# Weight sums rounded one piece later, and both plain products first in the first Strassen branch

## The chip, the cores and the metric

The kernel runs on one core of a Trainium2 chip, as one program. Its time is the device time in microseconds. The times of the kernel before are 688.67, 688.81 and 691.49 us, median 688.81; about half a per cent is what a measurement of it can tell from no change. Engines are called as in the profile: PE (matmul), DVE (VectorE), ACT (ScalarE), POOL (GpSimd) and SP, which issues the loads. Each works through its own queue in order, and semaphores tie them together.

## The reference

Three layers, one after the other, on 1152 tokens of 512 features:

```
q_pool = mean of pairs of q rows;  attn = softmax(q_pool k^T / 8) v      2 x 8 heads, 1152 x 64
h = x @ w_in;  g = elu(h);  x = g @ w_out                                512 -> 2048 -> 512
xn = x / rms(x) * rms_g                                                  last layer from here
out = (silu(xn @ w_gate) * (xn @ w_val)) @ w_out                         512 -> 1536 -> 512
```

The weights come as float64 and nearly float32 accuracy is kept.

## The kernel before, in words

Every float32 operand is split into a high part (rounded to the format that PE reads) and a low part (the rest), and a product is three matmuls: high by high, high by low, low by high (`product`, `group`). Activations lie transposed, features on the partitions, in three chunks `c` of 384 tokens; a PSUM bank holds 128 features of one chunk. Seven banks are used in turn.

**Weight pieces.** All weight matrices are read as one stream of pieces of 128 x 512 numbers (`Stream`). One piece goes through SP (load `wr`, two buffers), ACT (`we`, `wm`: two passes over the words of the float64), DVE (three passes that clamp, shift and join them into `wt`; L123, L125, L128), ACT again (high part `wh`, L176) and POOL (low part `wl`, L64). `Stream.work` is a generator; each `ws.step(i, k)` in the main program issues up to k more of these instructions between the matmuls, and so sets their place in each engine's queue. `wm` has a single PSUM bank, so ACT's next `wm` waits for DVE's `wt`.

**Gate and value products.** The last layer's first two products are made of 24 pieces, numbered 32 + 2n and 33 + 2n for n from 0 to 11; even n are gate, odd n value. n = 0 and 1 are multiplied plainly (`unit`). From n = 2 each pair of pieces is one `Branch`: chunks 0 and 1 together go through a Strassen-Winograd scheme with seven products m1 to m7 of half the depth (6 matmuls each, `group`, L707), and chunk 2 plainly, as m8 and m9 (12 matmuls each, `product`, L209 to L211). That is 66 matmuls. m3, m5, m6 and m7 read sums and differences of the four quarters of the pair: `combine` makes them on POOL (four adds into `sf`), `round` gives their high part on ACT (`sh` or `tsh`, L163) and their low part on POOL (`sl` or `tsl`, L64). In the trace `tsh` and `tsl` are a shared tile; they hold sums of pairs 3, 4, 6, 7 and so on beside differences of the activations.

DVE makes `u2` = m6 + m1 (L754) and `u3` = that + m7, still on the bank (L759); m7 is accumulated on m6's bank and so has to wait for `u2`, and m4 on m7's and has to wait for `u3`. The results go through silu on ACT (gate) or a multiplication on DVE (value, L717).

**Order.** `run` gives the order of the products by a list, with 3 steps of the stream behind each m1 to m7 and 6 behind m8 and m9. The first branch runs m1, m8, m6, then m5, m9, m7, m2; later ones are interleaved with what is left of the branch before. Ahead of the branches stand the norm of chunk 2 (`norms[2]`: `spread` transposes a reciprocal on PE, L633; `scale` on DVE, L639, with the parts `xh` on ACT and `xl` on POOL and DVE) and the four plain units.

The names in the rows: `b` is a bank, `u` a result or an add's output, `m` the copy of m1, `sf` a sum, `ts` and `s` its parts, `x` the activations.

Of the kernel before, what the change touches and what calls it, by code (L numbers as in the profile page):

```python
# [39 lines left out]
def tile_kernel(ctx: ExitStack, tc: tile.TileContext, qd, kd, vd, w1d, w2d, wgd, wvd, wod, rgd, outd):  # L40
# [33 lines left out]
    class Stream:  # L74


        def __init__(self, srcs):
            self.srcs = srcs
            self.loaded = self.done = self.at = 0
            self.alloc = False  # L80
            self.bank = self.late = None
            self.pairs_from, self.pairs, self.limit, self.pair = len(srcs), 0, 0, None
            self.raw, self.parts, self.sums = {}, {}, {}
            self.pools = [(wp, NE)]
            self.ops = self.work()
# [14 lines left out]
        def work(self):  # L100
            tail = None
            for i in range(len(self.srcs)):
                if tail and not wide:
                    yield from tail
                self.load(i + 2)
                w = self.raw.pop(i)
                if wide:

                    lo, hi = w[:, :, 0], w[:, :, 1]
                    e = wp.tile([128, 512], U32, tag="we", name="we", bufs=2)
                    w = wp.tile([128, 512], U32, tag="wt", name="wt", bufs=3)
                    t = self.bank.tile([128, 512], U32, tag="wm", name="wm", bufs=1) if self.bank else w
                    T.activation(out=e, in_=lo, func=AF.Copy, scale=0.93625 * 2.0 ** -29)
                    yield
                    T.activation(out=f(t), in_=f(hi), func=AF.Abs, scale=2.0 ** 16)  # L119
                    yield  # L120
                    if tail:
                        yield from tail
                    V.tensor_scalar(out=f(t), in0=f(t), scalar1=LEAST64, scalar2=MOST64, op0=ALU.max, op1=ALU.min)  # L123
                    yield
                    V.scalar_tensor_tensor(out=t, in0=t, scalar=3, in1=e,  # L125
                                           op0=ALU.logical_shift_left, op1=ALU.bitwise_or)
                    yield
                    V.scalar_tensor_tensor(out=w, in0=hi, scalar=0x80000000, in1=t,  # L128
                                           op0=ALU.bitwise_and, op1=ALU.bitwise_xor)
                    self.load(i + 3)  # L130
                    yield
                    w = f(w)
                if self.late:
                    yield from self.late
                    self.late = None
                tail = self.split(i, w)
                n, odd = divmod(i - self.pairs_from, 2)
                if 2 <= n < self.pairs:
                    tail = chain(tail, self.combine(n, even, w)) if odd else tail
                    even = w  # L140
                yield
            yield from tail

        def combine(self, n, a, b):

            sf = mp.tile([128, 4, 256], F32, tag="sf", name="sf", bufs=1)
            s1, s2, s3, s4 = (sf[:, k] for k in range(4))
            a11, a12, a21, a22 = a[:, 0:256], a[:, 256:512], b[:, 0:256], b[:, 256:512]
            G.tensor_tensor(out=s1, in0=a21, in1=a22, op=ALU.add)
            yield  # L150
            G.tensor_tensor(out=s2, in0=s1, in1=a11, op=ALU.subtract)
            yield
            G.tensor_tensor(out=s3, in0=a11, in1=a21, op=ALU.subtract)
            yield
            G.tensor_tensor(out=s4, in0=a12, in1=s2, op=ALU.subtract)
            self.late = self.round(n, sf.rearrange("p s (k c) -> p (s k) c", k=2))

        def round(self, n, sf):
            self.pair = n
# [53 lines left out]
    def xchunk(c):  # L213
        return lambda k: (xh[:, k, cs(c)], xl[:, k, cs(c)])
# [3 lines left out]
    def flush():  # L218
        while pending:
            pending.pop(0)()  # L220
# [230 lines left out]
    for n in range(ns):  # L451
        p, k = n // NPT, n % NPT
# [71 lines left out]
    for step in range(ns):  # L524
# [20 lines left out]
        for u in jobs.get(step, []):  # L545
            do_prep(u, (ACT[0], lo_pool) if step < 4 and u[0] != "q" else POOL)
            n = order.index(u)
# [40 lines left out]
    def bank():  # L588

        nonlocal nbank  # L590
        n, nbank = nbank % 7, nbank + 1
        if n == 5 and len(psb) == 1:
            with tc.using_default_side("right"):
                psb.append(ctx.enter_context(tc.tile_pool(name="psC", bufs=2, space=PSUM)))
                ws.bank = ctx.enter_context(tc.tile_pool(name="psW", bufs=1, space=PSUM))
        return psb[n >= 5].tile([128, 512], F32, tag="b", name="b", bufs=2 if n >= 5 else 5)[:, 0:CH]
# [47 lines left out]
    norms = [Norm(c) for c in range(3)]  # L644
# [3 lines left out]
    for hf in range(2):  # L648
# [30 lines left out]
        if hf:  # L679
            T.activation(out=dummy, in_=eps, func=AF.Sqrt)  # L680
            for c in range(3):
                for n in range(4):
                    m, q = 2 + n // 2, n % 2
                    if q == 0:
                        b = bank()
# [10 lines left out]
    class Branch:  # L696


        def __init__(self, n):
            self.n, self.val = n, n % 2  # L700
            self.i = 2 * (n // 2)
            self.w = [ws.get(wi + 2 * n + k) for k in range(2)]

# [6 lines left out]
        def out(self, k, c, p, add=None, into=None):  # L710
# [7 lines left out]
            else:  # L718
                pending.append(lambda: T.activation(out=d, in_=p, func=AF.Silu))

        def m(self, n):
            w = self.w
            a11, a12, a22 = ([t[:, 2 * j:2 * j + 2] for t in w[i]] for i, j in ((0, 0), (0, 1), (1, 1)))
            b11, b21, b22 = ([t[:, 2 * j:2 * j + 2, cs(l)] for t in (xh, xl)] for j, l in ((0, 0), (1, 0), (1, 1)))
            s = lambda k: [t[:, 2 * k - 2:2 * k] for t in ws.get_sums(self.n)]
            if n == 1:
                self.a = bank()
                self.group(self.a, a11, b11, True, False)
                self.m1 = hp.tile([128, CH], F32, tag="e", name="m1", bufs=4)
                T.copy(self.m1, self.a)  # L730
                flush()
            elif n == 2:
                self.group(self.a, a12, b21, False, True)
                flush()
                self.out(0, 0, self.a)
                self.out(1, 1, self.e, self.u3, self.a)
            elif n == 3:
                self.group(self.e, s(4), b22, False, True)
                flush()
                self.out(0, 1, self.e, self.u2)  # L740
            elif n == 4:
                self.group(self.b, a22, ts[3], False, True)
                flush()
                self.out(1, 0, self.b, self.m1)
            elif n == 5:
                self.e = bank()
                self.group(self.e, s(1), ts[0], True, False)
                flush()
            elif n == 6:
                self.b = bank()  # L750
                self.group(self.b, s(2), ts[1], True, False)
                flush()
                self.u2 = hp.tile([128, CH], F32, tag="e", name="u2", bufs=4)
                V.tensor_tensor(out=self.u2, in0=self.b, in1=self.m1, op=ALU.add)  # L754
            elif n == 7:
                self.group(self.b, s(3), ts[2], False, False)
                flush()
                self.u3 = up.tile([128, CH], F32, tag="u3", name="u3", bufs=2)
                V.tensor_tensor(out=self.u3, in0=self.b, in1=self.m1, op=ALU.add)  # L759
            else:  # L760
                b = bank()
                product(b, w[n - 8], xchunk(2), True, True)
                flush()
                self.out(n - 8, 2, b)

    def unit(i, c, between=None):
        b = bank(), bank()
        for n in range(2):
            product(b[n], ws.get(2 * n + i + wi), xchunk(c), True, True)
            if between and n == 0:  # L770
                between()
        return i, c, *b

    def swiglu(i, c, pg, pv, k=4):
        s = u[c][:, i]
        T.activation(out=s, in_=pg, func=AF.Silu)
        ws.step(wi, k)
        V.tensor_tensor(out=s, in0=pv, in1=s, op=ALU.mult)
# [21 lines left out]
    swiglu(*first[0], 0)  # L800
    lo_pool(ts[1][1], t2, ts[1][0])
    swiglu(*first[1], 2)
    units = [unit(1, 0, norms[2].spread)]
    norms[2].scale()
    lo_pool(ts[3][1], t4, ts[3][0])
    ws.step(wi, 7)
# [17 lines left out]
    def run(order, i, limit, k=3):  # L824
        ws.limit = limit
        for br, m in order:
            br.m(m)
            ws.step(wi + 2 * i, 2 * k if m > 7 else k)
# [15 lines left out]
    old = None  # L844
    for n in range(2, 11):
        b = Branch(n)
        if old:
            run([(b, 1), (old, 4), (b, 6), (old, 3)], n - 1, n + 2)
        else:
            run([(b, 1), (b, 8), (b, 6)], n, n + 2)  # L850
        if n == 10:
            split_u(0, 0, 3)
        run([(b, k) for k in ((5, 8, 7, 2, 9) if old else (5, 9, 7, 2))], n, n + 3)
        old = b
    b = Branch(11)
    run([(b, 1), (old, 4), (b, 6), (old, 3)], 10, 12, 1)
# [86 lines left out]
```

## Time and profile before

| | us |
|---|---|
| median of three runs | 688.81 |
| the profiled execution | 690.5 |
| its span | 688.6 |
| PE busy | 670.8 |
| DVE / ACT / POOL busy | 469.7 / 461.5 / 406.8 |

The span is the time between the first and last instruction that the profile sees; 1.9 us lie around it. Mean granted clock of PE over the span is 0.995 of full speed. In a timeline, the brackets at the end of a row give the idle time ahead of the instruction and what ended it. Matmuls are pipelined: each shows about 0.34 us, but the next starts half that later.

### The profile page before, as it was taken

What the parts mean: (1) busy time and instruction counts of PE and PEld (TensorE: products, weight loads), DVE (VectorE), ACT (ScalarE), POOL (GpSimd) and SP (SyncE); (2) the same over time, 40 slices, a digit from 0 to 9 for tenths busy, and PEclk for the clock granted to TensorE, in tenths of its full rate; (3) what the DMA queues carried; (4) which work ended last, traced back from release to release, by engine and by line L of the source; (5) the groups of instructions that cost most, each with busy time, mean ns of one, the idle gap of its engine ahead of it and who ended that gap; (6) DMA issues with size and microseconds to landing.
All of it is one profiled execution on the core that took longest, in us unless ns stands there. A gap on an engine that the chain in (4) does not pass through costs nothing.

```text
span 688.6 us, 11381 instructions
## 1 busy us (share of the span) xinstructions
PE 670.8 (97%) x4183; PEld 660.3 (96%) x4183; DVE 469.7 (68%) x803; ACT 461.5 (67%) x921; POOL 406.8 (59%) x366
## 2 busy tenths in 40 slices
PE   7999999999999999999999999999798999999997
PEld 6999999999999999999999999999698999999997
DVE  5989989998998966663445665397566866776300
ACT  5978889898988958984558875345655555644300
POOL 5798888888988406772224554376777676323200
PEclk9999999999999999999999999999999999999999
DMA  5522343223242001233222122101333222304200
GB/s 190 192 93 87 123 139 105 96 88 118 88 137 83 1 3 61 93 122 123 93 92 90 64 93 92 62 30 62 105 110 123 89 96 83 102 1 133 89 35 35
DMA packets 21608, 62.34 MB, mean 91 GB/s; under 512 B 2736, under 2 KB 4784, under 8 KB 21552
## 3 DMA queue, kind: packets, MB, share of 16 engines
q1 hardware_dynamic: 21552, 61.62, 27.1%
q8 instruction: 33, 0.54, 0.3%
q14 instruction: 23, 0.19, 0.1%
HBM read 59.25 MB, written 2.36 MB: 89 GB/s over the span
## 4 chain that ended last, share of the span: by engine, by line
PE 85%; POOL 4%; DVE 4%; ACT 3%; issue 2%; DMA 1%; SPq 0%; DVEq 0%; POOLq 0%; ACTq 0%
PE b L209 15%; PE b L211 15%; PE b L210 15%; PE s L321 10%; PE o L365 10%; PE b L707 10%; PE t L339 9%; DMA rawk<-in_k_dram 1%; DVE x L791 1%; POOL kd L64 1%; POOL vd L64 1%; DVE wm L125 1%; ACT xh L640 1%; DVE wm L123 1%; DVE wt L128 1%
## 5 line engine op out<-in xcount | busy, mean ns | idle before, releaser
L64 POOL TENSOR_TENSOR wl<-wt,wh 128x512 fp32r<-128x512 f32 x68 | 91.3, 1342 | 94.2 <-ACT wh L176 94.0
L209 PE MATMUL b<-xh,wh 128*128 128x384 f32 x356 | 120.5, 338 | 3.1 <-DVE u L717 3.1
L211 PE MATMUL b<-xh,wl 128*128 128x384 f32 x356 | 120.3, 338 | 0.0
L210 PE MATMUL b<-xl,wh 128*128 128x384 f32 x356 | 120.2, 338 | 0.0
L70 DVE TENSOR_TENSOR ptl<-t,pth 128x384 fp32r<-128x384 f32 x216 | 106.6, 548 | 4.4 <-ACT pth L347 3.5
L325 DVE TENSOR_SCALAR_CACHE_REDUCE p<-s 128x1152 f32<-128x1152 f32 x72 | 97.3, 1353 | 17.9 <-PE s L321 17.4
L347 ACT CAST pth<-t 128x384 fp32r<-128x384 f32 x216 | 89.2, 487 | 24.2 <-PE t L339 23.4
L321 PE MATMUL s<-kd,qt 128*128 128x384 f32 x480 | 97.9, 341 | 2.7 <-DVE p L325 1.6
L330 ACT ACTIVATE p<-p,st 128x1152 f32<-128x1152 f32 x72 | 91.5, 1271 | 0.5 <-DVE p L325 0.2
L339 PE MATMUL t<-ident,p 128*128 128x128 f32 x648 | 85.4, 275 | 1.4 <-ACT p L330 0.9
L321 PEld LDWEIGHTS s<-kd,qt 128*128 128x128 f32 x480 | 81.7, 188 | 4.5 <-POOL kd L64 2.0
L365 PE MATMUL o<-pth,vd 128*128 128x256 f32 (+1 forms) x288 | 84.4, 315 | 0.0
L339 PEld LDWEIGHTS t<-ident,p 128*128 128x128 f32 x648 | 73.9, 141 | 7.8 <-DVE ptl L70 4.7
L123 DVE TENSOR_SCALAR wm<-wm 128x512 f32<-128x512 f32 x62 | 43.1, 695 | 52.1 <-ACT wm L119 52.1
L365 PE MATMUL o<-ptl,vd 128*128 128x256 f32 (+1 forms) x288 | 78.4, 294 | 0.0
L209 PEld LDWEIGHTS b<-xh,wh 128*128 128x128 f32 x356 | 67.2, 189 | 3.4 <-DVE u L717 3.4
L210 PEld LDWEIGHTS b<-xl,wh 128*128 128x128 f32 x356 | 67.3, 189 | 0.0
L211 PEld LDWEIGHTS b<-xh,wl 128*128 128x128 f32 x356 | 67.3, 189 | 0.0
L64 POOL TENSOR_TENSOR gl<-e,gh 128x384 fp32r<-128x384 f32 x37 | 38.8, 1053 | 41.1 <-ACT gh L230 39.6
L209 PE MATMUL b<-gh,wh 128*128 128x384 f32 x180 | 60.9, 338 | 0.0
L211 PE MATMUL b<-gh,wl 128*128 128x384 f32 x180 | 60.5, 336 | 0.0
L210 PE MATMUL b<-gl,wh 128*128 128x384 f32 x180 | 60.5, 336 | 0.0
(183 smaller groups left out, 1510.7 us busy)
## 6 DMA issues: line engine op xcount, KB each, us to landing
wr<-in_w_dram SPq DMA_DIRECT2D x32, 512.0 KB, 3.3
rawk<-in_k_dram SPq DMA_DIRECT2D x32, 288.0 KB, 3.0
rawq<-in_q_dram SPq DMA_DIRECT2D x15, 576.0 KB, 4.1
wr<-in_wg_dram SPq DMA_DIRECT2D x12, 512.0 KB, 3.2
wr<-in_wv_dram SPq DMA_DIRECT2D x12, 512.0 KB, 3.2
wr<-in_wo_dram SPq DMA_DIRECT2D x12, 512.0 KB, 3.2
rawv<-in_v_dram SPq DMA_DIRECT2D x16, 288.0 KB, 2.8
out_dram<-o SPq DMA_DIRECT2D x12, 192.0 KB, 1.8
```

Of the source, the lines that this page charges most:

```text
L64: G.tensor_tensor(out=o, in0=i, in1=f(h), op=ALU.subtract)
L70: V.tensor_tensor(out=o, in0=i, in1=f(h), op=ALU.subtract)
L209: PE.matmul(out, lhsT=wh[:, k, :], rhs=ah, start=first and k == 0, stop=False)
L210: PE.matmul(out, lhsT=wh[:, k, :], rhs=al, start=False, stop=False)
L211: PE.matmul(out, lhsT=wl[:, k, :], rhs=ah, start=False, stop=last and k == 3)
L321: PE.matmul(s[:, m, 0:384], lhsT=a, rhs=b[:, 384 * m:384 * m + 384], start=n == 0, stop=n == len(parts) - 1)
L325: V.tensor_scalar(out=pt, in0=s[:, :, 0:384], scalar1=-0.0625, scalar2=None, op0=ALU.mult, op1=ALU.min, accum_out=st[p][:, 0, TILES[i][4], :])
L330: T.activation(out=pt, in_=pt, func=AF.Exp, scale=-1.0, bias=st[p][:, 0, TILES[i][4], :], accum_out=st[p][:, 1, TILES[i][4], :])
L339: PE.transpose(ps[:, k, :], src[:, 128 * b:128 * b + 128], ident)
L347: T.copy(oh, re(ps))
L365: PE.matmul(self.o[:, 0:self.N], lhsT=v[:, b, :], rhs=(pth, ptl)[u][:, g["buf"], b, g["c0"]:320], start=self.n == 0, stop=self.n == 17)
L707: PE.matmul(out, lhsT=a[x][:, k, :], rhs=b[y][:, k, :], start=first and (k, x, y) == (0, 0, 0), stop=last and (k, x, y) == (1, 1, 0), skip ...
```

## The change

Three places. In `Stream`, `combine` leaves its rounding in `next` instead of `late`; the cast to the high part is now issued behind the next piece's tail (its `wh`), and the low part behind that piece's passes on DVE, so that it comes after the previous piece's `wl` on POOL and not before it. In the first branch m9 stands behind m8 in front of m6, and the order m5, 9, 7, 2 is now m5, m2, m7; the output that needs both m2 and m7 is issued when the later one is done (`both`); the next branch's m6 comes ahead of the first branch's m4. And the transposes of the last norm stand behind both products of the unit in which they stood in the middle.

```
@@ -78,7 +78,7 @@
             self.srcs = srcs
             self.loaded = self.done = self.at = 0
             self.alloc = False
-            self.bank = self.late = None
+            self.bank = self.late = self.next = None
             self.pairs_from, self.pairs, self.limit, self.pair = len(srcs), 0, 0, None
             self.raw, self.parts, self.sums = {}, {}, {}
             self.pools = [(wp, NE)]
@@ -102,6 +102,9 @@
             for i in range(len(self.srcs)):
                 if tail and not wide:
                     yield from tail
+                    if self.next:
+                        yield from self.next
+                        self.next = None
                 self.load(i + 2)
                 w = self.raw.pop(i)
                 if wide:
@@ -120,6 +123,11 @@
                     yield
                     if tail:
                         yield from tail
+                    if self.late:
+                        yield next(self.late)
+                        yield next(self.late)
+                    self.late, late = self.next, self.late
+                    self.next = None
                     V.tensor_scalar(out=f(t), in0=f(t), scalar1=LEAST64, scalar2=MOST64, op0=ALU.max, op1=ALU.min)
                     yield
                     V.scalar_tensor_tensor(out=t, in0=t, scalar=3, in1=e,
@@ -130,9 +138,8 @@
                     self.load(i + 3)
                     yield
                     w = f(w)
-                if self.late:
-                    yield from self.late
-                    self.late = None
+                    if late:
+                        yield from late
                 tail = self.split(i, w)
                 n, odd = divmod(i - self.pairs_from, 2)
                 if 2 <= n < self.pairs:
@@ -153,7 +160,7 @@
             G.tensor_tensor(out=s3, in0=a11, in1=a21, op=ALU.subtract)
             yield
             G.tensor_tensor(out=s4, in0=a12, in1=s2, op=ALU.subtract)
-            self.late = self.round(n, sf.rearrange("p s (k c) -> p (s k) c", k=2))
+            self.next = self.round(n, sf.rearrange("p s (k c) -> p (s k) c", k=2))
 
         def round(self, n, sf):
             self.pair = n
@@ -697,7 +704,7 @@
 
 
         def __init__(self, n):
-            self.n, self.val = n, n % 2
+            self.n, self.val, self.half = n, n % 2, 0
             self.i = 2 * (n // 2)
             self.w = [ws.get(wi + 2 * n + k) for k in range(2)]
 
@@ -717,6 +724,11 @@
                 V.tensor_tensor(out=d, in0=p, in1=d, op=ALU.mult)
             else:
                 pending.append(lambda: T.activation(out=d, in_=p, func=AF.Silu))
+
+        def both(self):
+            self.half += 1
+            if self.half == 2:
+                self.out(1, 1, self.e, self.u3, self.a)
 
         def m(self, n):
             w = self.w
@@ -733,7 +745,7 @@
                 self.group(self.a, a12, b21, False, True)
                 flush()
                 self.out(0, 0, self.a)
-                self.out(1, 1, self.e, self.u3, self.a)
+                self.both()
             elif n == 3:
                 self.group(self.e, s(4), b22, False, True)
                 flush()
@@ -757,6 +769,7 @@
                 flush()
                 self.u3 = up.tile([128, CH], F32, tag="u3", name="u3", bufs=2)
                 V.tensor_tensor(out=self.u3, in0=self.b, in1=self.m1, op=ALU.add)
+                self.both()
             else:
                 b = bank()
                 product(b, w[n - 8], xchunk(2), True, True)
@@ -800,7 +813,8 @@
     swiglu(*first[0], 0)
     lo_pool(ts[1][1], t2, ts[1][0])
     swiglu(*first[1], 2)
-    units = [unit(1, 0, norms[2].spread)]
+    units = [unit(1, 0)]
+    norms[2].spread()
     norms[2].scale()
     lo_pool(ts[3][1], t4, ts[3][0])
     ws.step(wi, 7)
@@ -845,12 +859,12 @@
     for n in range(2, 11):
         b = Branch(n)
         if old:
-            run([(b, 1), (old, 4), (b, 6), (old, 3)], n - 1, n + 2)
+            run([(b, 1), (old, 4), (b, 6), (old, 3)] if n > 3 else [(b, 1), (b, 6), (old, 4), (old, 3)], n - 1, n + 2)
         else:
-            run([(b, 1), (b, 8), (b, 6)], n, n + 2)
+            run([(b, 1), (b, 8), (b, 9), (b, 6)], n, n + 2)
         if n == 10:
             split_u(0, 0, 3)
-        run([(b, k) for k in ((5, 8, 7, 2, 9) if old else (5, 9, 7, 2))], n, n + 3)
+        run([(b, k) for k in ((5, 8, 7, 2, 9) if old else (5, 2, 7))], n, n + 3)
         old = b
     b = Branch(11)
     run([(b, 1), (old, 4), (b, 6), (old, 3)], 10, 12, 1)
```

ACT in the first branch, before: `tsh` is the high part of the sums of pair 3, the cast that waits for POOL; `m_5849` is the copy of the first branch's m1.

```order
L176 CAST wh<-wt 128x512
L730 COPY m_5849<-b 128x384
L163 CAST tsh<-sf 128x1024
L117 ACTIVATE we<-wr 128x512
L119 ACTIVATE wm<-wr 128x512
L719 ACTIVATE u_5746<-b 128x384
L176 CAST wh<-wt 128x512
```

And now:

```order
L183 CAST wh<-wt 128x512
L742 COPY m_5849<-b 128x384
L120 ACTIVATE we<-wr 128x512
L122 ACTIVATE wm<-wr 128x512
L183 CAST wh<-wt 128x512
L726 ACTIVATE u_5746<-b 128x384
L170 CAST tsh<-sf 128x1024
```

The cast has moved behind the next piece's `we` and `wm` and the `wh` that follows, and an output's silu.

DVE in the same place, before: three rows are one piece; the adds that take `m_5849` are `u2` and then `u3` of the first branch.

```order
L123 TENSOR_SCALAR wm<-wm 128x512
L125 SCALAR_TENSOR_TENSOR wm<-wm,we 128x512
L128 SCALAR_TENSOR_TENSOR wt<-wr,wm 128x512
L754 TENSOR_TENSOR u_5883<-b,m_5849 128x384
L123 TENSOR_SCALAR wm<-wm 128x512
L125 SCALAR_TENSOR_TENSOR wm<-wm,we 128x512
L128 SCALAR_TENSOR_TENSOR wt<-wr,wm 128x512
L759 TENSOR_TENSOR u_5932<-b,m_5849 128x384
```

And now:

```order
L131 TENSOR_SCALAR wm<-wm 128x512
L133 SCALAR_TENSOR_TENSOR wm<-wm,we 128x512
L136 SCALAR_TENSOR_TENSOR wt<-wr,wm 128x512
L131 TENSOR_SCALAR wm<-wm 128x512
L133 SCALAR_TENSOR_TENSOR wm<-wm,we 128x512
L136 SCALAR_TENSOR_TENSOR wt<-wr,wm 128x512
L766 TENSOR_TENSOR u_5906<-b,m_5849 128x384
L131 TENSOR_SCALAR wm<-wm 128x512
L771 TENSOR_TENSOR u_5943<-b,m_5849 128x384
```

`u2` has gone from behind the first of these pieces to behind the second; between `u2` and `u3` stands one row instead of three.

POOL at the first sums, before: four adds, the sums' low part, two pieces' low parts.

```order
L149 TENSOR_TENSOR sf<-wt 128x256
L151 TENSOR_TENSOR sf<-sf,wt 128x256
L153 TENSOR_TENSOR sf<-wt 128x256
L155 TENSOR_TENSOR sf<-wt,sf 128x256
L64 TENSOR_TENSOR sl<-sf,sh 128x1024
L64 TENSOR_TENSOR wl<-wt,wh 128x512 x2
```

And now:

```order
L156 TENSOR_TENSOR sf<-wt 128x256
L158 TENSOR_TENSOR sf<-sf,wt 128x256
L160 TENSOR_TENSOR sf<-wt 128x256
L162 TENSOR_TENSOR sf<-wt,sf 128x256
L64 TENSOR_TENSOR wl<-wt,wh 128x512
L64 TENSOR_TENSOR sl<-sf,sh 128x1024
L64 TENSOR_TENSOR wl<-wt,wh 128x512
```

The sums' low part stands between the two pieces' low parts.

## Rows read from the trace of the kernel before

**Rows 1.** Page: span, busy times, and PE in 40 slices of 17.2 us

```profile
span 688.6 us, 11381 instructions
...
PE 670.8 (97%) x4183; PEld 660.3 (96%) x4183; DVE 469.7 (68%) x803; ACT 461.5 (67%) x921; POOL 406.8 (59%) x366
...
PE   7999999999999999999999999999798999999997
```

**Rows 2.** Windows: length, busy PE, PEld, DVE, ACT, POOL (count), granted clock, DMA, GB/s

```profile
486.50:490.00 3.50, 3.50 (x22) 3.35 (x20) 3.05 (x6) 1.58 (x4) 2.21 (x3) 1.00 0.45 149
497.67:501.70 4.03, 4.03 (x14) 4.03 (x15) 3.25 (x6) 2.25 (x6) 3.18 (x4) 0.60 0.47 146
540.00:560.00 20.00, 20.00 (x116) 20.00 (x115) 14.05 (x25) 10.67 (x19) 14.53 (x14) 1.00 0.26 89
```

**Rows 3.** PE timeline, 466 to 519: start, length, line, tiles, idle before and releaser

```profile
466.33 0.54 PE L633 MATMUL b<-ident,rr 128*128 128x128 f32 x3 [0.60 <-DVE rr L627]
...
473.17 0.34 PE L210 MATMUL b<-xl,wh 128*128 128x384 f32 x1
...
486.08 0.45 PE L707 MATMUL b<-tsh,sl 128*128 128x384 f32 x1 [1.10 <-POOL sl L64]
...
490.72 0.44 PE L707 MATMUL b<-tsh,sh 128*128 128x384 f32 x1 [0.55 <-DVE u L754]
...
497.67 0.45 PE L707 MATMUL b<-tsh,wh 128*128 128x384 f32 x1 [3.51 <-DVE u L759]
...
518.38 0.44 PE L209 MATMUL b<-xh,wh 128*128 128x384 f32 x1 [3.12 <-DVE u L717]
```

**Rows 4.** Waits of all engines: total us, times, longest

```profile
DVE wm L123 <- ACT wm L119: 52.1, 35, 5.4
```

**Rows 5.** ACT timeline, 482 to 513, first two branches

```profile
484.41 0.63 ACT L119 ACTIVATE wm<-wr 128x512 f32<-128x512 f32 x1
...
492.78 1.05 ACT L163 CAST tsh<-sf 128x1024 fp32r<-128x1024 f32 x1 [3.91 <-POOL sf L155]
...
512.88 1.05 ACT L163 CAST sh<-sf 128x1024 fp32r<-128x1024 f32 x1 [4.31 <-POOL sf L155]
```

**Rows 6.** DVE timeline, 470 to 518

```profile
470.26 2.18 DVE L639 SCALAR_TENSOR_TENSOR x<-x,rg,b 128x384 f32<-128x384 f32 x4
...
478.26 1.42 DVE L70 TENSOR_TENSOR xl<-x,xh 128x768 fp32r<-128x768 f32 x1 [1.51 <-ACT xh L810]
...
481.58 0.69 DVE L128 SCALAR_TENSOR_TENSOR wt<-wr,wm 128x512 uint32<-128x512 uint32 x1
...
486.60 0.69 DVE L128 SCALAR_TENSOR_TENSOR wt<-wr,wm 128x512 uint32<-128x512 uint32 x1
...
494.94 0.70 DVE L123 TENSOR_SCALAR wm<-wm 128x512 f32<-128x512 f32 x1 [4.27 <-ACT wm L119]
...
497.07 0.55 DVE L759 TENSOR_TENSOR u<-b,m 128x384 f32<-128x384 f32 x1
...
517.77 0.56 DVE L717 TENSOR_TENSOR u<-b,u 128x384 f32<-128x384 f32 x1
```

**Rows 7.** POOL timeline, 471 to 504

```profile
471.49 2.31 POOL L64 TENSOR_TENSOR xl<-x,xh 128x384 fp32r<-128x384 f32 x2 [4.77 <-ACT xh L640]
...
478.82 1.46 POOL L149 TENSOR_TENSOR sf<-wt 128x256 f32<-128x256 f32 x1
...
481.75 0.74 POOL L155 TENSOR_TENSOR sf<-wt,sf 128x256 f32<-128x256 f32 x1
483.64 2.38 POOL L64 TENSOR_TENSOR sl<-sf,sh 128x1024 fp32r<-128x1024 f32 x1 [1.16 <-ACT sh L163]
...
496.23 1.27 POOL L64 TENSOR_TENSOR wl<-wt,wh 128x512 fp32r<-128x512 f32 x1
...
503.77 2.41 POOL L64 TENSOR_TENSOR tsl<-sf,tsh 128x1024 fp32r<-128x1024 f32 x1 [1.16 <-ACT tsh L163]
```

**Rows 8.** Loads of the weight pieces, tile wr: issue to landing

```profile
DMA to landing us min/median/max: 3.0/3.2/6.1
```

More of the change, by code (lines that the diff above doesn't have):

```diff
@@ L80, in __init__ @@
             self.alloc = False
-            self.bank = self.late = None
+            self.bank = self.late = self.next = None
             self.pairs_from, self.pairs, self.limit, self.pair = len(srcs), 0, 0, None
@@ L104, in work @@
                     yield from tail
+                    if self.next:
+                        yield from self.next
+                        self.next = None
                 self.load(i + 2)
@@ L122, in work @@
                         yield from tail
+                    if self.late:
+                        yield next(self.late)
+                        yield next(self.late)
+                    self.late, late = self.next, self.late
+                    self.next = None
                     V.tensor_scalar(out=f(t), in0=f(t), scalar1=LEAST64, scalar2=MOST64, op0=ALU.max, op1=ALU.min)
@@ L132, in work @@
                     w = f(w)
-                if self.late:
-                    yield from self.late
-                    self.late = None
+                    if late:
+                        yield from late
                 tail = self.split(i, w)
@@ L155, in combine @@
             G.tensor_tensor(out=s4, in0=a12, in1=s2, op=ALU.subtract)
-            self.late = self.round(n, sf.rearrange("p s (k c) -> p (s k) c", k=2))
+            self.next = self.round(n, sf.rearrange("p s (k c) -> p (s k) c", k=2))
         def round(self, n, sf):
@@ L699, in __init__ @@
         def __init__(self, n):
-            self.n, self.val = n, n % 2
+            self.n, self.val, self.half = n, n % 2, 0
             self.i = 2 * (n // 2)
@@ L719, in out, with both @@
                 pending.append(lambda: T.activation(out=d, in_=p, func=AF.Silu))
+        def both(self):
+            self.half += 1
+            if self.half == 2:
+                self.out(1, 1, self.e, self.u3, self.a)
         def m(self, n):
@@ L735, in m @@
                 self.out(0, 0, self.a)
-                self.out(1, 1, self.e, self.u3, self.a)
+                self.both()
             elif n == 3:
@@ L759, in m @@
                 V.tensor_tensor(out=self.u3, in0=self.b, in1=self.m1, op=ALU.add)
+                self.both()
             else:
@@ L802, in tile_kernel @@
     swiglu(*first[1], 2)
-    units = [unit(1, 0, norms[2].spread)]
+    units = [unit(1, 0)]
+    norms[2].spread()
     norms[2].scale()
@@ L847, in tile_kernel @@
         if old:
-            run([(b, 1), (old, 4), (b, 6), (old, 3)], n - 1, n + 2)
+            run([(b, 1), (old, 4), (b, 6), (old, 3)] if n > 3 else [(b, 1), (b, 6), (old, 4), (old, 3)], n - 1, n + 2)
         else:
-            run([(b, 1), (b, 8), (b, 6)], n, n + 2)
+            run([(b, 1), (b, 8), (b, 9), (b, 6)], n, n + 2)
         if n == 10:
             split_u(0, 0, 3)
-        run([(b, k) for k in ((5, 8, 7, 2, 9) if old else (5, 9, 7, 2))], n, n + 3)
+        run([(b, k) for k in ((5, 8, 7, 2, 9) if old else (5, 2, 7))], n, n + 3)
         old = b
```

## The prediction

> **What bounds the kernel now.** I read the engine totals and the PE slices first. PE is busy 670.8 of 688.6 us and the only slices after the start that are not at 9 are 28 and 30, so from 482 to 534 us; everything before and after them is a full PE [rows 1]. Then the windows: in an undisturbed stretch of the branches 116 matmuls go by in 20 us, 0.1724 us each, at a granted clock of 1.00; behind the longest gap 14 matmuls take 4.03 us at 0.60, a mean over a low part at 1.2 GHz and a rest at 2.4 [rows 2]. Then PE's timeline, for every matmul with an idle time in brackets: the five gaps from the last norm on are 0.60, 1.10, 0.55, 3.51 and 3.12 us, in sum 8.88 [rows 3]. What a low clock adds: 14 matmuls should take 2.41 us, so 1.62 us are lost behind the 3.51 gap; behind the 3.12 gap the trace repeats that (14 matmuls in 4.02 us), 1.61. Together 12.1 us are lost in the stretch that the change touches. There is nothing else on PE to win: a faster side engine is worth only what it takes from these 12.1 us.
>
> Why PE waits there is read one engine back. DVE's wait on `wm` for ACT is a large group, 52.1 us in 35 waits [rows 4]. In ACT's timeline roundings of weight sums wait in turn for POOL's last add; the two that matter have 3.91 and 4.31 us of idle time ahead of them [rows 5]. ACT is strictly in order, so the next piece's `we` and `wm` stand behind the blocked cast; DVE's clamp waits 4.27 us for `wm`, and behind the clamp and its two partners stands the add `u3`, which PE's next group needs: it starts at 497.07 and PE at 497.67 [rows 3, 6]. The 3.12 gap is the same chain: cast 512.88, `u` at 517.77, PE at 518.38 [rows 3, 5, 6]. POOL itself is not full: lower parts of sums two pairs apart start at 483.64 and 503.77, 10.07 us for a pair [rows 7], of which work is four adds at 0.74, one lower part of a sum at 2.4 and two of pieces at 1.27, 7.9 us; the rest is waiting for ACT's rounding. A branch on PE is 66 matmuls, 11.4 us.
>
> **The change, step by step.** No instruction is added or removed; only the order moves, on PE, ACT, DVE and POOL, and SP's loads follow as buffers come free.
>
> *Rounding behind the next piece.* The cast of a sum now comes after the next piece's `we`, `wm` and the current `wh`, so POOL has long finished when ACT reaches it. ACT no longer stands still ahead of it, DVE gets its clamp, and the two long gaps go: 3.51 + 3.12, and with them the low clock, 1.62 + 1.61; 9.86 us in sum. POOL has `wl` to do while ACT rounds, so its 1.16 us wait [rows 7] falls away too, and its pair comes near to 7.9 us.
>
> *Price at the first sum.* The first pair has no lead. `wt` of piece 38 ends at 482.27 [rows 6]; then `wm` of 39 (0.6), `wh` of 38 (0.6), the cast (1.05) [rows 5], while POOL does `wl` of 38; the lower part starts about 484.9 and ends near 487.3, where it ended at 486.02 before [rows 7]. PE asked for it at 484.98 (486.08 less 1.10) and now, with the other plain product of 12 matmuls in front, 2.07 us later, and 0.2 us earlier for the norm: at about 486.85. The gap of 1.10 becomes 0.5; with a wake-up on either engine between I take 0.7, between 0.5 and 0.9. The product in front needs only piece 37 and the next of seven banks in turn, both long free, so it costs nothing itself.
>
> *What is late next: `u2` of the first branch.* This add held PE for 0.55 us before [rows 3]. It now stands on DVE behind piece 41's three instructions too. Chain: `wm` of 39 starts at 482.33, as soon as `wt` of 38 is done; from `wm` to the end of `wt` the rows give 2.88 us (484.41 to 487.29) [rows 5, 6], so `wt` of 39 ends at 485.2. That frees the load buffer for piece 41, which lands 3.2 us later (3.0 to 6.1) [rows 8], 488.5. Then `we` (0.6), `wm` to `wt` (2.88) and the add (0.55): 492.5. PE comes to that group 16 matmuls after 487.3, at 490.1. The gap grows from 0.55 to 2.4; with the load at 3.0 and the passes overlapped it is 1.9, with a load 0.7 later 3.1. Whether the clock falls behind it the trace can't say: behind 1.10 us it stayed at 1.00, behind 3.51 it fell [rows 2, 3]. I take no fall and keep 1.6 us for the range.
> The Trainium skill (TensorE: Matmul & The Clock Gate, section HAM oscillation) says that matmuls after a long enough wait run at the low clock again; the trace agrees, 0.60 behind 3.51 us. [...]
>
> *The third sum's lead.* POOL: the first lower part ends 487.3, `wl` of 39, four adds, `wl` of 40, lower part: 487.3 + 7.9 = 495.2. PE wants it in the next branch's m6 at about 495.0: a gap of 0.3, up to 0.6. After that POOL gains 11.4 - 7.9 = 3.5 us on PE with each branch, so no later branch waits for a sum. m4 of the first branch, moved behind the next branch's m6, has 12 matmuls, 2.1 us, between m7 and itself, which cover `u3`; the output add that now waits for both m2 and m7 is the same instruction in a later place, and nothing on PE waits for it. SP carries only the loads here, so none stands behind a later one.
>
> *Norm's transposes after the whole unit.* They waited 0.60 us for a reciprocal; 12 matmuls now run ahead of them. But PE then comes to the third chunk at 472.5 instead of 473.17, and POOL's first lower part of it ends at 472.65 (half of 2.31 after 471.49) [rows 3, 7]; with a second such wait 0.4 us come back (0.2 to 0.5). DVE's scaling begins at 470.26 behind DVE's other work [rows 6], 2 us after the moved transposes, so nothing else moves.
>
> **The sum.** Lost before 12.1. Lost after: 0.4 + 0.7 + 2.4 + 0.3 = 3.8, clock 0. Gain 8.3 us, and with the ends of the terms 12.1 - 2.7 = 9.4 at best, 12.1 - 5.1 - 1.6 = 5.4 at worst. The profiled execution took 690.5 us (688.6 span and 1.9 around it), so 682.2; the median of the runs shown, 688.81, is 1.7 below. If profiling costs those 1.7, the forecast is 680.5; if the median run lacked one of the two low-clock stretches, 1.6 of the gain isn't there and it is 682.1. I take 681.0, nearer the first. That case's own range is 679.4 to 682.3.
>
> **Rivals.**
> *A: the first branch keeps a gap with a low clock.* `u2` waits 3.1 us and the clock falls: 0.7 + 1.6 less gain, 680.5 + 2.3 = 682.8, and up to 684.5 with a branch more. For it: the chain to `u2` now runs through a DMA landing, and the longest landing is 6.1 us [rows 8]. Against: the median is 3.2.
> *B: the waits return a branch later.* If DVE stays behind through the denser stream, one gap of 3.1 with 1.6 of clock comes back at the third branch: 680.5 + 4.7 = 685.2, at the edge of no change. For it: DVE's adds stand between the pieces' instructions as before. Against: what made DVE late was ACT's stand of 3.91 and 4.31 us [rows 5], and that is gone by the order.
> *C, slower: POOL becomes the bound.* More POOL work now lies beside DVE. The first add of a sum took 1.46 us beside DVE's `xl` (478.26, both inputs in SBUF) and 0.74 alone [rows 6, 7]. If all of a pair went so, 7.9 would become 15.8 us against PE's 11.4, 4.4 us in each of nine branches, 40 us: 720. It decides from 11.4 us for a pair. Against: `wl` beside piece instructions at 496.23 took 1.27 [rows 7], and in the branches DVE's instructions take one operand from a PSUM bank.
> The Trainium skill (GPSIMD Engine Reference, Key points) says that GpSimd shares its SBUF interfaces with VectorE and contends with instructions that have two SBUF inputs; the 1.46 beside `xl` agrees, and by that rule C would need such instructions inside the branches.
>
> **Numbers.** Forecast 0.65, A 0.20, B 0.09, C 0.03, and 0.03 for a loss that none of these names. A measurement of this kernel tells about 0.5% (3.4 us) from no change. Faster by more (below 685.4): forecast, A, most of B less a margin, 0.90; same 0.06; slower 0.04. The range 679.0 to 684.6 holds the forecast with 0.4 below for durations that come from one execution, and A.
>
> **What would show it.** Right: in the profile after, ACT's cast of a sum with no idle time of 4 us ahead of it, POOL's pairs at about 8 us in the first branches, one PE gap near 2.4 us released by the first branch's `u2`, one below 1 us at the first sum, none in the branches after the second, and no slice of PE below 8 but one. Wrong: a gap of 3 us or more behind a DVE `u` of a later branch, a POOL pair above 11 us, or a granted clock near 0.6 behind the `u2` gap (then A).

## The result, and the profile after

The changed kernel took 682.88 us in the median of four runs (681.77 to 683.45) against 688.89 of the kernel before (four runs, 688.67 to 691.49): ratio 0.9902, interval 0.9876 to 0.9929. Timed once more beside further kernels it took 681.41 (six runs, 680.65 to 682.99) against 690.28 (eleven runs, 688.10 to 691.49): 0.9881, interval 0.9862 to 0.9900. It is faster by 6.0 us by the one and 8.9 by the other. The eleven runs of the kernel before lie in two groups, four at 688.10 to 688.91 us and seven at 690.25 to 691.49, at mean granted clocks that overlap (0.993 to 0.995 and 0.989 to 0.995); what parts them is open, and how many of each a median holds is part of what lies between 6.0 and 8.9.

The page of the profile after, in the same lines as [rows 1]: the span, the busy times, PE's slices, now of 17.0 us.

```profile
span 681.2 us, 11377 instructions
...
PE 669.6 (98%) x4183; PEld 659.5 (97%) x4183; DVE 469.1 (69%) x803; ACT 462.5 (68%) x921; POOL 406.9 (60%) x366
...
PE   7999999999999999999999999999899999999997
```

One slice of the two dips is left, at 8. PE's timeline there (start, length, line, tiles, idle before and releaser) answers to [rows 3]:

```profile
472.60 0.33 PE L216 MATMUL b<-xh,wh 128*128 128x384 f32 x1
472.87 0.44 PE L217 MATMUL b<-xl,wh 128*128 128x384 f32 x1
473.15 0.34 PE L218 MATMUL b<-xh,wl 128*128 128x384 f32 x1
...
487.58 0.44 PE L714 MATMUL b<-tsh,sl 128*128 128x384 f32 x1 [0.45 <-POOL sl L64]
...
493.22 0.69 PE L714 MATMUL b<-tsh,sh 128*128 128x384 f32 x1 [2.58 <-DVE u L766]
493.70 0.52 PE L714 MATMUL b<-tsl,sh 128*128 128x384 f32 x1
```

Of the five gaps two are left in brackets: 0.45 us at the first sum and 2.58 at the first branch's m7, which waits for `u2` (L766 now). At the third chunk the starts show two small ones without a bracket: 0.27 and 0.28 us between starts where 0.17 is the rule, 0.2 us together. The windows row of the stretch behind the long gap (length, busy PE, PEld, DVE, ACT, POOL with counts, granted clock, DMA, GB/s), as in [rows 2], in this profile and then in a second one of the same kernel, whose own gap there is 2.64 us:

```profile
493.22:497.25 4.03, 4.03 (x15) 4.03 (x16) 2.37 (x4) 2.38 (x6) 4.03 (x3) 0.61 0.40 130
```

```profile
487.52 0.44 PE L714 MATMUL b<-tsh,sl 128*128 128x384 f32 x1 [0.45 <-POOL sl L64]
...
493.21 0.44 PE L714 MATMUL b<-tsh,sh 128*128 128x384 f32 x1 [2.64 <-DVE u L766]
```

```profile
493.21:497.24 4.03, 4.03 (x23) 4.03 (x24) 2.75 (x5) 3.62 (x8) 4.03 (x3) 1.00 0.42 130
```

In the first, 15 matmuls go by in 4.03 us instead of 2.59: the clock is at the 1.2 GHz level for most of it, and 1.44 us are lost. In the second, 23 go by at 1.00. So what is lost after is 0.45 + 2.58 + 0.2 + 1.44 = 4.7 of 12.1 us, or 0.45 + 2.64 + 0.2 = 3.3. The spans say the same: 688.6 before, 681.2 and 679.7 after, 7.4 and 8.9 less, where 12.1 - 4.7 = 7.4 and 12.1 - 3.3 = 8.8.

The mean granted clock of a whole execution, which every run has (0.995 in the first profile, 1.000 in the second), doesn't say where the clock was low. In the first profile it was low in a second place too, near 10 us, far ahead of all that the change touches. The same windows row, from 0 to 20 us, in the first profile and then in the second:

```profile
0.00:10.00 10.00, 6.85 (x31) 6.37 (x32) 3.59 (x13) 2.83 (x4) 3.18 (x10) 0.91 0.76 255
10.00:20.00 10.00, 8.68 (x48) 7.50 (x48) 8.26 (x14) 9.27 (x18) 9.36 (x10) 0.91 0.30 99
```

```profile
0.00:10.00 10.00, 7.65 (x36) 7.17 (x36) 4.37 (x14) 2.83 (x4) 3.27 (x10) 1.00 0.76 251
10.00:20.00 10.00, 8.29 (x50) 6.66 (x49) 7.84 (x15) 9.65 (x19) 9.50 (x10) 1.00 0.31 106
```

Nearly nothing of that one is left at the first sum, where PE starts at 487.58 in the one and 487.52 in the other, so the sums above stand.

The other engines of the first profile: ACT's casts of the sums (`sh`, `tsh`) and one load of the pieces; DVE's last pass of piece 41 and `u2`; POOL's low parts of sums; the wait on `wm`.

```profile
483.71 1.05 ACT L170 CAST sh<-sf 128x1024 fp32r<-128x1024 f32 x1
...
488.90 0.68 ACT L120 ACTIVATE we<-wr 128x512 uint32<-128x512 uint32 x1 [0.86 <-DMA wr<-in_wg_dram]
...
491.94 1.05 ACT L170 CAST tsh<-sf 128x1024 fp32r<-128x1024 f32 x1 [0.92 <-POOL sf L162]
...
508.02 1.05 ACT L170 CAST sh<-sf 128x1024 fp32r<-128x1024 f32 x1 [0.47 <-POOL sf L162]
```

```profile
492.01 0.69 DVE L136 SCALAR_TENSOR_TENSOR wt<-wr,wm 128x512 uint32<-128x512 uint32 x1 [0.44 <-POOL sf L162]
492.61 0.55 DVE L766 TENSOR_TENSOR u<-b,m 128x384 f32<-128x384 f32 x1
```

```profile
485.14 2.39 POOL L64 TENSOR_TENSOR sl<-sf,sh 128x1024 fp32r<-128x1024 f32 x1
...
493.09 2.38 POOL L64 TENSOR_TENSOR tsl<-sf,tsh 128x1024 fp32r<-128x1024 f32 x1
...
500.92 2.42 POOL L64 TENSOR_TENSOR tsl<-sf,tsh 128x1024 fp32r<-128x1024 f32 x1
```

```profile
DVE wm L131 <- ACT wm L122: 41.5, 26, 5.4
```

The three casts shown wait 0, 0.92 and 0.47 us where 3.91 and 4.31 stood [rows 5]. POOL's low parts of sums start 7.95 and 7.83 us apart, where it was 10.07 [rows 7]. The wait of 52.1 us [rows 4] is 41.5. DVE's `u2` starts at 492.61, and two waits tell why it isn't sooner: ACT's `we` of piece 41 waited 0.86 us for its load, and DVE's last pass waited 0.44 us for POOL's last add of the second sum, which reads the buffer that the pass writes.

### The profile page after: what moved, and what is told of

It is laid out like the page before. It is cut to its first block, busy times and chain, and to the rows that moved or that the text cites. A ratio compares the mean times of both kernels' runs of the same rounds, so it can differ in the third digit from the quotient of the medians.

```text
span 681.2 us, 11377 instructions
## 1 busy us (share of the span) xinstructions
PE 669.6 (98%) x4183; PEld 659.5 (97%) x4183; DVE 469.1 (69%) x803; ACT 462.5 (68%) x921; POOL 406.9 (60%) x366
## 4 chain that ended last, share of the span: by engine, by line
PE 87%; POOL 3%; DVE 3%; ACT 3%; DMA 2%; issue 1%; SPq 1%; POOLq 0%; DVEq 0%; ACTq 0%
PE b L216 15%; PE b L218 15%; PE b L217 15%; PE s L328 10%; PE b L714 10%; PE o L372 10%; PE t L346 10%; DMA rawk<-in_k_dram 1%; DVE x L804 1%; POOL kd L64 1%; POOL vd L64 1%; ACT xh L647 1%; ACT p L337 1%; PE t L407 1%; DMA wr<-in_wg_dram 0%
## 5 line engine op out<-in xcount | busy, mean ns | idle before, releaser
L328 PEld LDWEIGHTS s<-kd,qt 128*128 128x128 f32 x480 | 83.1, 191 | 5.2 <-DVE kd L70 2.3
L131 DVE TENSOR_SCALAR wm<-wm 128x512 f32<-128x512 f32 x62 | 43.1, 694 | 41.5 <-ACT wm L122 41.5
L120 ACT ACTIVATE we<-wr 128x512 uint32<-128x512 uint32 x68 | 45.4, 668 | 25.3 <-DMA wr<-in_wo_dram 13.5
```

Source lines behind the costliest of these rows:

```text
L328: PE.matmul(s[:, m, 0:384], lhsT=a, rhs=b[:, 384 * m:384 * m + 384], start=n == 0, stop=n == len(parts) - 1)
```

## The experiments

Each is compared with the kernel before on the same chip; the first four ran on one chip, where the kernel before has 690.16 us (17 runs), the last three on another, where it has 690.28 (11 runs).

**The rounding alone.** The changed `Stream`; everything below it as before.

```
-    units = [unit(1, 0)]
-    norms[2].spread()
+    units = [unit(1, 0, norms[2].spread)]
-            run([(b, 1), (b, 8), (b, 9), (b, 6)], n, n + 2)
+            run([(b, 1), (b, 8), (b, 6)], n, n + 2)
-        run([(b, k) for k in ((5, 8, 7, 2, 9) if old else (5, 2, 7))], n, n + 3)
+        run([(b, k) for k in ((5, 8, 7, 2, 9) if old else (5, 9, 7, 2))], n, n + 3)
...
```

> The changed rounding of weight sums alone: the order of the products and the place of the norm's transposes are those of the kernel before. Theory (the blocked cast was the cause of both long gaps): neither the 3.51 nor the 3.12 us gap is there; PE asks for the first sum's low part at about 485.0 as before, and it ends near 487.5 as in the changed kernel (its row there: 485.14 + 2.39), so one gap of about 2.4 us stands at the first sum in place of the 0.45 there, and no 2.58 us gap at u2. Lost idle time 0.6 + 2.4, with or without 1.4 us of low clock behind: 681.5 to 683.5, within 1 us of the changed kernel. Rival (the order of the first branch is half of the gain): a gap of 2 us or more at u2 or u3 comes on top, 685 to 686.

Measured: 680.73 us (679.69 to 682.00, five runs), ratio 0.987, interval 0.9851 to 0.9889. Its PE timeline from the last norm on, all rows with an idle time, and the window behind the longer one:

```profile
465.63 0.54 PE L640 MATMUL b<-ident,rr 128*128 128x128 f32 x3 [0.60 <-DVE rr L634]
...
486.52 0.44 PE L714 MATMUL b<-tsh,sl 128*128 128x384 f32 x1 [2.13 <-POOL sl L64]
```

```profile
486.52:490.50 3.98, 3.98 (x23) 3.98 (x24) 3.46 (x6) 2.56 (x6) 3.77 (x5) 1.00 0.41 141
```

The 0.60 is back, the first sum costs 2.13, and nothing else on PE waits in the branches; the clock stayed up in this profile. It is 0.8 us below the expectation's range, and with 2.7 us of idle time in brackets against 3.0 and 3.1 not behind the whole change. The theory holds: the rounding is the gain, and the order of the products and the moved transposes, both left out here, add none to it.

**The order alone.** The changed order and the moved transposes over the old `Stream`.

```
-                    if late:
-                        yield from late
+                if self.late:
+                    yield from self.late
+                    self.late = None
...
-            self.next = self.round(n, sf.rearrange("p s (k c) -> p (s k) c", k=2))
+            self.late = self.round(n, sf.rearrange("p s (k c) -> p (s k) c", k=2))
```

> The changed order of the products and the place of the norm's transposes alone, with the rounding of before. Theory (the blocked cast): ACT still stands 3.9 us ahead of the second sum's cast; u2 of the first branch now stands behind the piece that this cast blocks, so the 0.55 and the 3.51 us gaps become one of 6 to 8 us at u2, the 3.1 us gap at the third branch stays, and the gap at the first sum goes: 688 to 691, no gain. Rival (the order with both plain products in front does the work): the first gaps shrink to below 1 us, 684 to 686.

Measured: 689.23 us (688.01 to 690.05, twelve runs), ratio 0.999, interval 0.998 to 1.000. PE's rows with an idle time, and ACT's cast of the second sum:

```profile
488.55 0.44 PE L707 MATMUL b<-xh,wh 128*128 128x384 f32 x1 [0.35 <-ACT m L735]
...
497.60 0.69 PE L707 MATMUL b<-tsh,sh 128*128 128x384 f32 x1 [7.74 <-DVE u L759]
...
518.29 0.44 PE L209 MATMUL b<-xh,wh 128*128 128x384 f32 x1 [0.80 <-DVE u L717]
```

```profile
492.36 1.04 ACT L163 CAST tsh<-sf 128x1024 fp32r<-128x1024 f32 x1 [3.86 <-POOL sf L155]
```

The cast still stands 3.86 us, and the 1.10, 0.55 and 3.51 us gaps have become one of 7.74 at `u2` (L759 in this file). I expected the 3.12 us gap to stay; it ends at 518.29, where it ended at 518.38 before, but PE comes to it later and waits 0.80. The three brackets make 8.89 us, the five of before 8.88, and the time is the same within 1 us.

**`u2` early.** The changed kernel, with the stream's steps behind the first branch's m9 moved behind its m6.

```
-            run([(b, 1), (b, 8), (b, 9), (b, 6)], n, n + 2)
+            run([(b, 1), (b, 8)], n, n + 2)
+            run([(b, 9)], n, n + 2, 0)
+            run([(b, 6)], n, n + 2, 9)
```

> The changed kernel, but the 6 steps of the stream behind the first branch's m9 come behind its m6, so that u2 stands ahead of the next piece on DVE. Theory A (u2 behind the piece is what the 2.58 us gap costs): the gap goes, and with it 1.4 us of low clock: 682.9 - 4.0 = 678.9. Theory B (PE only waits there for what it would wait for a little later): the second sum's low part ends at 495.47 in the changed kernel whatever PE does, so the next branch's m6, which is then due near 492.9, waits about 2.5 us for it; the time stays at 681.5 to 683, with the low clock moved there.

Measured: 682.47 us (682.19 to 683.24, five runs), ratio 0.9893, interval 0.9876 to 0.9909. PE's rows with an idle time, POOL's low part of the second sum, and the window behind the last gap:

```profile
488.00 0.45 PE L714 MATMUL b<-tsh,sl 128*128 128x384 f32 x1 [0.46 <-POOL sl L64]
...
493.38 0.44 PE L714 MATMUL b<-tsh 128*128 128x384 f32 x1 [0.19 <-ACT tsh L170]
...
495.87 0.45 PE L714 MATMUL b<-tsh,tsl 128*128 128x384 f32 x1 [1.87 <-POOL tsl L64]
```

```profile
493.43 2.38 POOL L64 TENSOR_TENSOR tsl<-sf,tsh 128x1024 fp32r<-128x1024 f32 x1
```

```profile
495.87:499.50 3.63, 3.63 (x13) 3.63 (x14) 2.65 (x6) 2.29 (x4) 3.55 (x5) 0.59 0.21 59
```

Theory B holds. The gap at `u2` is gone, and 0.19 + 1.87 us stand at the next branch's m6 instead, released by the low part that ends at 495.81, with a low clock (0.59) behind. `u2` holds PE hardly longer than the second sum does: of its 2.58 us, 2.06 are waited for there.

**The gap filled.** 13 matmuls more, ahead of the first branch's m7, into a bank that nothing reads.

```
             elif n == 7:
+                if self.n == 2:
+                    fill = bank()
+                    for k in range(13):
+                        PE.matmul(fill, lhsT=w[0][0][:, 0, :], rhs=xh[:, 0, cs(0)], start=k == 0, stop=k == 12)
```

> The changed kernel with 13 further matmuls ahead of the first branch's m7, into a bank that nothing reads, so that PE works through most of its 2.58 us wait for u2. Theory (the low clock is what the gap itself brings): the granted clock stays at 1.00 behind it, the rest of the gap is about 0.3 us, and 1.4 us are saved: 681.4. But POOL's second sum, which ends at 495.47, is then the later one: up to 0.9 us of it come back at the next branch's m6. Rival (the clock falls for another reason, or the filling costs its own time): 682.9 or above, with a clock near 0.6 between 493 and 497.

Measured: 681.08 us (680.07 to 681.22, four runs), ratio 0.9867, interval 0.9848 to 0.9885. PE's rows with an idle time, and the window behind:

```profile
487.31 0.44 PE L714 MATMUL b<-tsh,sl 128*128 128x384 f32 x1 [0.45 <-POOL sl L64]
...
492.92 0.44 PE L714 MATMUL b<-tsh,sh 128*128 128x384 f32 x1 [0.30 <-DVE u L766]
```

```profile
492.92:496.95 4.03, 4.03 (x23) 4.03 (x24) 2.63 (x5) 3.63 (x8) 4.03 (x3) 1.00 0.42 130
```

The rest of the gap is 0.30 us, and 23 matmuls go by at 1.00; the mean granted clock of its runs is 1.000, 1.000, 1.000 and 0.999. m7 starts 5.61 us behind the first sum's matmul, where it was 5.64. Of the 1.8 us between this span (679.4) and that of the first profile of the changed kernel (681.2) 0.3 lie ahead of the first sum (487.31 against 487.58), and 1.4 are the clock's. To the changed kernel timed later (681.41) there is hardly a difference: there four of six runs have a mean granted clock of 1.000 without any filling (last experiment). So these four runs alone don't show that it was the filling that kept the clock up.

**The transposes put back.** The changed kernel with `units = [unit(1, 0, norms[2].spread)]`.

> The changed kernel with the norm's transposes back in the middle of the unit. Theory (what is saved ahead of a wait that another engine sets is only waited later): the 0.60 us gap at the transposes returns, the gap at the first sum shrinks from 0.45 to about 0.2 and u2 comes at the same time as before, so the 2.58 us gap ends where it did: the same time within 0.3 us, 682.7 to 683.2. Rival (the 0.60 us is a gain of its own, as the prediction's sum has it, less 0.4): 683.1 to 683.6 and every later gap unchanged in size.

Measured: 681.29 us (680.88 to 683.01, five runs), ratio 0.9881, interval 0.9860 to 0.9902. PE's rows with an idle time:

```profile
466.87 0.54 PE L640 MATMUL b<-ident,rr 128*128 128x128 f32 x3 [0.60 <-DVE rr L634]
...
487.81 0.44 PE L714 MATMUL b<-tsh,sl 128*128 128x384 f32 x1 [0.20 <-POOL sl L64]
...
493.20 0.69 PE L714 MATMUL b<-tsh,sh 128*128 128x384 f32 x1 [2.35 <-DVE u L766]
```

0.60 + 0.20 + 2.35 = 3.15 us against 0.45 + 2.64 + 0.2 = 3.3, and m7 starts at 493.20 against 493.21 and 493.22. What is saved at the norm is waited for later; this part of the change is worth nothing here. The time is 1.4 us below the range expected, 682.7 to 683.2, which was built on the 682.88 of the changed kernel; timed beside it that one has 681.41.

**Both branches eased.** `u2` early as above, and the second branch's m8 ahead of its m6, its m2 ahead of its m7.

```
-            run([(b, 1), (old, 4), (b, 6), (old, 3)] if n > 3 else [(b, 1), (b, 6), (old, 4), (old, 3)], n - 1, n + 2)
+            run([(b, 1), (old, 4), (b, 6), (old, 3)] if n > 3 else [(b, 1), (b, 8), (b, 6), (old, 4), (old, 3)], n - 1, n + 2)
-        run([(b, k) for k in ((5, 8, 7, 2, 9) if old else (5, 2, 7))], n, n + 3)
+        run([(b, k) for k in ((5, 8, 7, 2, 9) if n > 3 else (5, 2, 7, 9) if old else (5, 2, 7))], n, n + 3)
```

> The changed kernel with u2 early (steps of the stream behind the first branch's m6 and not behind m9), and the second branch's first plain product m8 ahead of its m6, its m2 ahead of its m7. Theory (what PE waits for is POOL's second sum, which ends at about 495.5 whatever stands in front): 12 matmuls, 2.1 us, that need no sum now stand ahead of the wait, so that 2.58 + the low clock becomes one gap of 0.5 to 0.9 at the second branch's m6, at most one of 0.6 at the first branch's last product that waits for an add, clock 1.00: 682.9 - 1.4 - 1.3 = 680.2. Rival (the wait moves on once more, to m7 of the second branch behind its own u2 or to the third sum): a gap of about 2 us there, 682 to 683.

Measured: 679.33 us (678.81 to 680.16, five runs), ratio 0.9845, interval 0.9823 to 0.9866. PE's rows with an idle time, and the window of the first branches:

```profile
488.27 0.44 PE L714 MATMUL b<-tsh,sl 128*128 128x384 f32 x1 [0.46 <-POOL sl L64]
...
496.17 0.45 PE L714 MATMUL b<-tsh,tsl 128*128 128x384 f32 x1 [0.30 <-POOL tsl L64]
```

```profile
488.27:520.00 31.73, 31.43 (x177) 30.80 (x178) 26.06 (x46) 23.32 (x42) 31.38 (x29) 1.00 0.41 141
```

Two gaps of 0.46 and 0.30 us are left; the granted clock of its runs is 1.000 in four and 0.999 in one. It is 2.1 us below the changed kernel beside it, the best of the kernels run. With 12 matmuls that need no sum (2.1 us) ahead of the one that does, and `u2` early, most of the wait of 2.64 us is gone. `u2` early alone, above, moved the wait and did not remove it; the 12 matmuls alone were not run.

**The changed kernel again.**

> The changed kernel itself once more, beside the kernel before and the two below. Against the kernel before at 690.2 (17 runs of the first experiments, where the record of it stood at 688.9): if that was drift of the chip, the changed kernel moves up with it, to 684; if the first few runs of before happened to be low, it stays at 682.9. Theory of the low clock behind the 2.58 us gap: its mean granted clock is 0.997 or less in every run, where the kernel whose gap was filled had 1.000 or 0.999 in all four, and the time is 1.4 to 1.8 above that one's 681.1.

Measured: 681.41 us, as above. Its six runs have a mean granted clock of 1.000 in four (680.65 to 681.51 us) and 0.997 and 0.995 in two (682.99 and 682.13). So the expectation that the clock falls in every run was wrong, though the wait is the same (2.64 us; its row and its window stand above). In the eleven runs of the kernel before it is 0.989 to 0.995 throughout. Where in those two runs the clock was low their means can't say: in the first profile it was at the start as well as behind `u2`, and with the transposes put back a run at 0.997 took 681.12 us, no longer than those at 1.000 (680.88 and 681.29). The kernel before stands at 690.3 again, so the first four runs of it happened to be low; the changed kernel did not move up with it.

## Why the prediction was right

The time forecast was 681.0, the range 679.0 to 684.6, and the times are 682.88 and 681.41. The reason it gave is the one that the experiments show: ACT's cast stood ahead of POOL's sum, and all of the gain comes with moving it.

Step by step, with the times of the first and the second profile. *Rounding behind the next piece*: both long gaps are gone, with their low clock, and POOL's pair is 7.83 to 7.95 us (7.9 said). *First sum*: 0.45 where 0.7 was taken. *`u2`*: 2.58 and 2.64 where 2.4 was taken; the load of piece 41 stands in its chain, as said (ACT waited 0.86 us for it), but 0.44 us is a wait that the chain left out, DVE's last pass for POOL's adds on the same buffer. *Low part of the second sum*: no gap of its own, where 0.3 was taken: it ends at 495.47 in the first profile, and PE, held at `u2`, comes to it at 497.19 there and at 495.78 in the second. *Norm*: 0.2 us at the third chunk where 0.4 was taken. The sum, 3.8 us lost, was 3.3 without the low clock.

```profile
497.19 0.34 PE L714 MATMUL b<-tsh,tsl 128*128 128x384 f32 x1
```

```profile
495.78 0.34 PE L714 MATMUL b<-tsh,tsl 128*128 128x384 f32 x1
```

The low clock was the open term. The prediction took no fall and gave rival A, with a fall, 682.8 to 684.5. Both happen: of the ten runs of the changed kernel the four with a mean granted clock of 1.000 took 680.65 to 681.51 us, at the forecast, and the six at 0.995 to 0.997 took 681.77 to 683.45, towards A. The first median, 682.88, lies in A's range and outside the forecast case's own (679.4 to 682.3), and by the prediction's own sign, a granted clock near 0.6 behind the `u2` gap, the first profile is A's; the second median and profile are the forecast's. So a fall was likelier than A's 0.20. A's other half, a wait of 3.1 us at `u2` through a late load, did not come. The Trainium skill (TensorE: Matmul & The Clock Gate, Part 1: The HAM clock gate) says that how many matmuls run at the low clock at a kernel's start varies between runs of one kernel; these runs agree, with a granted clock of 0.91 over the first 10 us of one and 1.00 in another. Behind a wait in the middle of the kernel they show the same, 15 matmuls in 4.03 us in one and 23 in the other. B and C did not come either: no gap in later branches, and a POOL pair of 7.83 us where C needs 11.4.

Two readings were wrong. The profiled execution's 1.7 us above the median were put down to the profiler or to a low clock that the median run lacked. The runs give no sign of either: none of the 28 later runs of the kernel before has a mean granted clock above 0.995, runs of 688.10 and of 690.28 us both have 0.995, and the median of the 28 is 690.2, where the profiled one was 690.5. That 681.0 came out so near to 681.41 is in part luck: from 690.28 the same gain of 8.3 us gives 682.0. The sum's gain of 8.3 us is 8.9 in the second measurement and 6.0 in the first. And the sum priced the parts of the change each by its own gaps, which says nothing of what a part is worth: the order of the products, the larger part of the diff, is worth nothing (680.73 without it), and the moved transposes nothing either, because POOL's first two sums, and `u2` in front of the second, set when PE may go on. Two slips change nothing: the best ends of the sum's terms add up to 2.6 us and not 2.7, and "nothing else on PE to win" passes over the last slice, at 7 before and after, which the change doesn't touch.

## What to carry to other kernels

A cast that waits in an in-order queue holds up everything behind it; give it the next independent work first, and look two engines on for who pays. Where several waits in a row are set by one stream on another engine, closing the one with the largest bracket moves it to the next; work that doesn't need the stream must be put ahead of the whole row. Two runs of a kernel with gaps of about 2 us can differ by a low clock, 1.4 us here, so a gap can cost more than its own length.

## What was not expected of the hardware

A wait of the same length on PE brought a low clock in one execution and none in another: behind 2.58 us 15 matmuls in 4.03 us at 0.61, behind 2.64 us in a later execution of the same kernel 23 at 1.00. Behind 2.13 us the clock stayed up in the profile shown, behind 0.19 + 1.87 it was 0.59. Over all runs: the kernels whose profiles show 2 us or more of waiting in the branches once the rounding is moved (the changed kernel with ten runs, the rounding alone, `u2` early and the transposes put back with five each) have a mean granted clock below 0.999 in 17 of 25 runs; the two with no gap there above 0.46 us (the gap filled, both branches eased) in none of nine. That ties most of the falls to the wait, though a mean can also hold one at the start; why a fall comes in one execution and not in the next stays open.
